# Whole-row loads and GpSimd-issued stores in place of paired-row loads and SP-issued stores, in a fused recurrent-unit and feed-forward kernel

## The chip, the cores and the metric

The kernel runs on one core of a Trainium2 chip. The metric is device time in microseconds (us), the median of several runs. The engines are named as in the profile: PE is TensorE, DVE is VectorE, ACT is ScalarE, POOL is GpSimd and SP is SyncE. A core moves data with 16 DMA engines; an engine's sequencer issues a transfer on its queue, and the transfer then runs beside the engines.

## The reference, cut to what matters

```
log_a = 8 * sigmoid(r_gate) * log(sigmoid(a_param))      # per channel
a     = exp(log_a)
g     = sqrt(max(1 - a*a, 1e-6)) * sigmoid(i_gate) * x
h[t]  = a[t] * h[t-1] + g[t]                             # over 5824 steps, 4 sequences
out   = (((h @ w1) * (h @ w2)) @ w3) @ w_out
```

The inputs x, r_gate and i_gate are float32 of 4 x 5824 x 256. The feed-forward weights are 256 x 1024 (w1, w2), 1024 x 1024 (w3) and 1024 x 256 (w_out). The output has 23,296 rows of 256 float32 numbers.

## The kernel before

**Chunks.** The 23,296 rows are worked through in 47 chunks: two of 256 rows, 44 of 512, and one of 256. The recurrence needs channels on partitions and time along the free dimension, while the inputs lie in memory with channels along a row. So each chunk is loaded by rows, the gate's tanh (`th_r`) and the gated input (`u_t`) are made in that layout as bf16, and both are turned. Chunks 0, 1, 2, 3, 4, 7 and 12 turn the gate on TensorE, and chunks 0 to 7 turn the input there (`turn_pe`, into PSUM tiles `ptr`); the others are turned by a DMA transpose that SP issues (`turn_dma`, L205, into `rt` and `ut`).

**Steps of a chunk.** In the order that data flows, with the letter that the kernel's order list uses:

- r, i, x (`load`, L142): three loads by SP, 512 KB each for a chunk of 512 rows.
- R, I (L150 and L160, ACT): tanh of both gates. p (L166, POOL): adds 1 to the input gate. t (L170, POOL, in two halves): multiplies it with x into `u_t`.
- V, U: the turns.
- d (`decay`, L209, ACT, once per 128 channels): `a_t` = exp of the turned gate. s (`square`, L220, POOL mostly): a times a into `nrm`. q (`root`, L230, ACT): the square root.
- g (`gated`, L235, DVE): `nrm` times the turned input. h (`scan`, L252, DVE, once per 128 channels): the recurrence, into `h_t`. y (`cast`, L267, POOL): `h_t` to bf16 `y_t`.
- a, b (L287 and L291, PE): the two up projections into PSUM. c (L302, ACT, some on DVE): a's result into `sa`. m (L308, DVE): the product with b's result, into `g_t`.
- D (`down`, L315, PE): the down projection, with w3 and w_out folded into one matrix at the start. e (`evac`, L327, ACT, some on DVE): the result from PSUM into `ot`, 256 rows at a time, in a ring of three tiles. o (`store`, L340): one transfer of 256 KB from `ot` to the output.

The last chunk has its own evacuation and store (`evac_last`, `store_last`, L331 and L336), in two transfers of 128 KB.

**Which rows lie where.** For chunks that both turns of which are on TensorE (`long_rows`: 0, 1, 2, 3, 4 and 7), a partition holds 4 (or 2) neighbouring rows, and decay and the gated product put time back in order with strided views. For all other chunks a partition holds pairs of neighbouring rows (`run(c)` is 2), that is, runs of 2 KB. After the turn the even and the odd rows then lie in separate blocks of 128 columns. `decay` reads these blocks densely and writes every second element of `a_t` (`paired`, `halves`). `gated` does the same in two instructions, one for each j, each of 128 x 512 elements for a chunk of 512 rows:

```
nc.sync.dma_start(
    out=t[:, :n, :].rearrange("p (h j) c -> p h j c", j=run(c)),
    in_=src[nm][starts[c]:starts[c] + sizes[c], :].rearrange("(h p j) c -> p h j c", p=P, j=run(c)))
...
a, pr = paired(a), halves(pr)
```

**Order of the work.** The kernel has its whole order written out by hand as a list of words (`ORDER`, L454). `o8.1` is the second store of chunk 8, `y11` the cast of chunk 11. Each word emits its instructions on its engine, and each engine and each queue works strictly in the order of the list. Waits between engines are made by semaphores, for data and for tiles of a ring that come free. So an instruction that waits holds up all that follow on its engine. Before the change, SP's queue carries everything that moves: loads, DMA transposes and stores.

Of the kernel before, what the change touches and what calls it, by code (L numbers as in the profile page):

```python
# [13 lines left out]
ALU = mybir.AluOpType  # L14
# [8 lines left out]
def kernel(  # L23
# [12 lines left out]
    nc = tc.nc  # L36
# [87 lines left out]
    def long_rows(c):  # L124
        return c in TURN_R and c in TURN_U

    def run(c):
        return sizes[c] // P if long_rows(c) else 2

    def paired(t):  # L130
        return t.rearrange("p (h q j) -> p h j q", q=P, j=2)

    def halves(t):
        return t.rearrange("p (h j q) -> p h j q", q=P, j=2)

# [6 lines left out]
    def load(c, nm):  # L142
        n = sizes[c] // P
        t = ring(loads, [P, 4, D], F32, name=nm + "_t", tag=nm)
        nc.sync.dma_start(
            out=t[:, :n, :].rearrange("p (h j) c -> p h j c", j=run(c)),
            in_=src[nm][starts[c]:starts[c] + sizes[c], :].rearrange("(h p j) c -> p h j c", p=P, j=run(c)))
        T[nm, c] = t
# [60 lines left out]
    def decay(c, cb):  # L209
# [4 lines left out]
        if long_rows(c):  # L214
            a, pr = in_time(a), turned(pr)
        else:
            a, pr = paired(a), halves(pr)
# [17 lines left out]
    def gated(c):  # L235
# [7 lines left out]
        for j in range(2):  # L243
            if w == CT:
                n = T["n", c].rearrange("p cb (x j) -> p j (cb x)", j=2)[:, j].rearrange("p (y q) -> p y q", q=P)
                pu = T["pu", c].rearrange("p cb (h j q) -> p j (cb h) q", q=P, j=2)[:, j]
            else:
                n = T["n", c][:, :, :w].rearrange("p cb (q j) -> p j cb q", j=2)[:, j]
                pu = T["pu", c][:, :, :w].rearrange("p cb (j q) -> p j cb q", q=P)[:, j]
            nc.vector.scalar_tensor_tensor(out=n, in0=n, scalar=1e-3, in1=pu, op0=ALU.max, op1=ALU.mult)  # L250
# [89 lines left out]
    def store(c, j2):  # L340
        t0 = starts[c] + 2 * j2 * P
        nc.sync.dma_start(out=out[t0:t0 + 2 * P, :].rearrange("(j p) c -> p j c", p=P),
                          in_=T["ot", c, j2])
# [89 lines left out]
    def last(c):  # L433
# [34 lines left out]
        b3.3 m3.2 m3.3 p5 a4.0.1 r9 a4.1.0 d5.0 d5.1 R8 d6.0 s6.0 s7.0 d6.1 p6 t5.0 p7 x6 x7 o0.0 a4.0.0 i10 V8 D2.0  # L468
        D2.1 c4.0.0 c4.1.0 b4.0 r10 o1.0 s5.0 s5.1 R9 s6.1 c4.0.1 s7.1 e2.0 m4.0 a4.2.0 a4.2.1 q7 V9 c4.2.0 a4.1.1
        c4.2.1 b4.1 t5.1 b4.2 c4.1.1 U5 a4.3.0 i8 o2.0 m4.1 D3.0 r11 t6.0 t6.1 U6 q5 q6 g5 h5.0 h5.1 c4.3.0 m4.2 i9 g6  # L470
        d8.0 a4.3.1 D3.1 D2.2 D2.3 b4.3 c4.3.1 d9.0 e3.0 y5 a5.1.0 t7.0 s8.0 b5.0 m4.3 e2.1 R10 d8.1 a5.0.0 a5.0.1
        h6.0 h6.1 a5.2.0 c5.1.0 D4.0 c5.0.0 c5.0.1 I8 m5.0 x8 a5.1.1 D4.1 c5.2.0 o3.0 I9 b5.1 a5.2.1 c5.1.1 b5.2 m5.1
        c5.2.1 R11 e4.0 p8 y6 m5.2 r12 I10 t7.1 a5.3.0 a6.0.0 U7 V10 c5.3.0 c6.0.0 d9.1 x10 r13 D3.2 g7 D3.3 e3.1
        a6.0.1 x9 t8.0 t8.1 a6.1.0 d10.0 d10.1 o2.1 V11 a6.1.1 a5.3.1 h7.0 h7.1 s9.0 c6.0.1 s9.1 c6.1.0 b6.0 R13 o4.0
        a6.2.1 a6.2.0 c5.3.1 c6.1.1 y7 m6.0 b5.3 s8.1 U8 D4.2 b6.1 a7.0.0 p9 p10 m5.3 t9.0 c6.2.0 b6.2 c6.2.1 R12 m6.1
        a6.3.0 q8 q9 D4.3 a6.3.1 c7.0.0 m6.2 c6.3.0 e4.1 t9.1 b6.3 c6.3.1 t10.0 t10.1 m6.3 V12 a7.0.1 g8 x11 h8.0 h8.1
        b7.0 a7.1.0 s10.0 d12.0 d12.1 c7.1.0 c7.0.1 D6.0 D6.1 m7.0 a7.2.0 D5.0 a7.1.1 D5.1 V13 d13.0 s13.0 i11 I11
        e6.0 o3.1 d11.0 y8 d11.1 e5.0 r15 c7.1.1 a7.2.1 b7.1 c7.2.0 c7.2.1 b7.2 U9 U10 i13 i12 r14 o4.1 x13 d13.1 o6.0
        a7.3.0 a7.3.1 a8.0.1 o5.0 m7.1 m7.2 R15 I13 a8.0.0 c8.0.0 b7.3 c8.0.1 c7.3.0 D6.2 c7.3.1 m7.3 p11 b8.1 s11.0
        D6.3 b8.0 a8.1.0 D5.2 D5.3 g9 h9.0 s10.1 s12.0 t11.0 i16 s11.1 R14 h9.1 e6.1 I12 c8.1.0 q10 p13 a8.1.1 c8.1.1  # L480
        m8.0 V15 q11 p12 y9 e5.1 m8.1 a8.3.0 D7.0 D7.1 V14 i15 o5.1 o6.1 r16 t13.0 t11.1 U11 r19 x12 a8.2.0 c8.2.0 g10
        h10.0 h10.1 c8.3.0 e7.0 y10 a8.2.1 d15.0 r17 b8.2 a8.3.1 b9.0 a9.0.0 c8.2.1 t13.1 m8.2 o7.0 x15 s15.0 a9.0.1
        D7.2 c8.3.1 c9.0.0 c9.0.1 I16 D7.3 m9.0 a9.1.0 d15.1 e7.1 b8.3 p16 a9.1.1 U13 m8.3 b9.1 a10.0.0 I15 a9.2.0
        c9.1.0 b9.2 c9.1.1 R16 a9.2.1 t12.0 p15 c10.0.0 d14.0 a9.3.0 a9.3.1 c9.2.0 s13.1 s14.0 d14.1 m9.1 D8.0 R17
        t12.1 c9.3.0 s12.1 c9.3.1 c9.2.1 V16 D8.1 D8.2 D8.3 a10.0.1 a10.2.0 m9.2 s15.1 e8.1 i14 r18 e8.0 c10.0.1 g11
        h11.0 h11.1 b10.0 a10.2.1 a10.1.0 y11 m10.0 b9.3 a10.1.1 b10.1 m9.3 c10.1.0 U12 x14 c10.2.0 d16.0 c10.1.1
        m10.1 d16.1 c10.2.1 a10.3.0 I14 a10.3.1 s16.0 b10.2 o8.1 s14.1 i19 c10.3.0 c10.3.1 R19 o7.1 a11.0.1 a11.0.0
        b10.3 t15.0 s16.1 a11.1.1 c11.0.0 c11.0.1 m10.2 m10.3 b11.0 x16 q12 m11.0 a11.1.0 c11.1.0 D10.0 a11.2.0 t15.1
# [136 lines left out]
```

## Time and profile before

| | |
|---|---|
| median of 3 runs | 521.21 us (520.61 to 521.88) |
| the profiled execution | 520.61 us, of which the profile's span is 518.8 us |
| granted TensorE clock | 1.0 |
| bytes moved by DMA | 123.82 MB, 239 GB/s in the mean |
| HBM read, written | 78.91 MB, 23.86 MB |
| median time to landing of a 512 KB load (r, i, x) | 5.4, 5.7, 5.4 us |
| median time to landing of a 256 KB store | 3.4 us |
| median time to landing of a DMA transpose | 4.4 us (rt), 4.3 us (ut) |

A row of the profile's groups reads: line, engine, operation, tile written and tiles read, shapes, count, then the busy time in us and the mean of one instruction in ns, then the idle time of the engine before these instructions and what ended it. A row of the waits reads: who waited for whom, us in total, times, and the longest. In the chain that ended last, the profile goes back from the last instruction to what released each one, and gives the share of the span by engine and line. A row of stretches reads: from and to, length, busy time and count of PE, weight loads, DVE, ACT and POOL, then the granted clock, the DMA engines' share and GB/s. Matmul ends are modelled, and matmuls overlap, so PE's busy time is not a measure of its peak.

The work of the start (loading weights and folding w3 with w_out) lasts until some 50 us; the first store is issued at 53.5 us and the last at 516.2 us.

### The profile page before, as it was taken

To read this page: it belongs to the slowest core of one execution; us is meant where nothing else is said; L and a number is where in the kernel's file an instruction comes from. 1 tells how busy PE (TensorE), PEld (TensorE's weight loads), DVE (VectorE), ACT (ScalarE), POOL (GpSimd) and SP (SyncE) were. 2 spreads that over 40 slices of the span, in tenths; PEclk is the share of its full clock that TensorE was granted. 3 is DMA by queue.
4 is the path that set the end of the run, shared out by engine and by line. 5 is a ranking of instruction groups with operands and counts; after the bars stand their busy time and mean duration, and the time that the engine had idled before them with its cause. 6 is when DMAs were issued, how large, how long until landed. Compare 5 with 4: busy or idle time off the path is not lost.

```text
span 518.8 us, 9105 instructions
## 1 busy us (share of the span) xinstructions
PE 501.7 (97%) x3267; PEld 313.9 (61%) x3321; DVE 443.1 (85%) x455; ACT 468.4 (90%) x720; POOL 310.2 (60%) x271
## 2 busy tenths in 40 slices
PE   7799999999999999999999999999999999999997
PEld 6658565566565566555656555565565655656566
DVE  4899999999999879989979699988989698859762
ACT  6999999999998999999999999998997969888553
POOL 1674858646637956866584993946645668480200
DMA  8996999999989998795998997989785896252112
GB/s 298 407 415 244 316 285 294 322 231 308 318 236 261 263 283 268 204 307 160 297 303 268 276 279 172 245 225 251 184 263 135 209 331 150 101 144 80 51 63 102
DMA packets 146178, 123.82 MB, mean 239 GB/s; under 512 B 86355, under 2 KB 110677, under 8 KB 146133
## 3 DMA queue, kind: packets, MB, share of 16 engines
q1 hardware_dynamic: 146128, 123.23, 82.6%
q8 instruction: 26, 0.43, 0.3%
q14 instruction: 20, 0.16, 0.1%
q10 hardware_dynamic: 4, 0.00, 0.0%
HBM read 78.91 MB, written 23.86 MB: 198 GB/s over the span
## 4 chain that ended last, share of the span: by engine, by line
PE 71%; ACT 10%; DVE 8%; DMA 5%; issue 4%; SPq 0%; ACTq 0%; DVEq 0%
PE po L323 24%; PE pb L284 23%; PE pa L284 22%; DMA wf<-in_moe_w_dram 4%; ACT sa L300 4%; DVE g_t L312 3%; DVE nrm L250 3%; ACT a_t L218 2%; DVE h_t L265 2%; PE pw L394 1%; DMA x_t<-in_x_dram 1%; ACT nrm L232 1%; ACT i_t L163 1%; ACT ot L300 1%; ACT th_r L156 1%
## 5 line engine op out<-in xcount | busy, mean ns | idle before, releaser
L312 DVE TENSOR_TENSOR g_t<-sa,pb 128x1024 bf16<-128x1024 bf16 (+1 forms) x188 | 218.5, 1179 | 53.5 <-PE pb L284 28.7
L284 PEld LDWEIGHTS <-w_sb 128*128 128x128 bf16 x1504 | 146.0, 98 | 152.1 <-issue 10.9
L300 ACT CAST sa<-pa 128x512 bf16<-128x512 f32 (+1 forms) x339 | 182.6, 589 | 30.3 <-PE pa L284 17.8
L284 PE MATMUL pa<-y_t,w_sb 128*128 128x512 bf16 (+1 forms) x721 | 185.9, 372 | 4.6 <-ACT sa L300 2.2
L284 PE MATMUL pb<-y_t,w_sb 128*128 128x512 bf16 (+1 forms) x729 | 182.7, 372 | 4.5 <-DVE g_t L312 2.6
L323 PE MATMUL po<-wp_sb,g_t 128*128 128x256 bf16 x1456 | 177.7, 273 | 0.6 <-ACT sa L300 0.3
L323 PEld LDWEIGHTS <-g_t 128*128 128x128 bf16 x1456 | 142.4, 98 | 40.6 <-issue 0.8
L274 POOL CAST y_t<-h_t 128x1024 bf16<-128x1024 f32 (+1 forms) x46 | 49.0, 1064 | 149.0 <-DVE h_t L265 116.0
L187 POOL TENSOR_TENSOR u_t<-i_t,x_t 128x512 bf16<-128x512 f32 (+1 forms) x89 | 121.7, 1384 | 6.9 <-DMA ut<-u_t 3.7
L265 DVE TENSOR_TENSOR_SCAN h_t<-a_t,h_t,nrm 128x512 f32<-128x512 f32 (+1 forms) x92 | 118.6, 1318 | 1.9
L228 POOL TENSOR_TENSOR nrm<-a_t 128x512 f32<-128x512 f32 (+1 forms) x74 | 81.0, 1113 | 13.2 <-ACT a_t L218 13.2
L250 DVE SCALAR_TENSOR_TENSOR nrm<-nrm,ut 128x512 f32<-128x512 f32 (+1 forms) x78 | 69.4, 931 | 5.6 <-ACT nrm L232 5.3
L218 ACT ACTIVATE a_t<-rt,la 128x512 f32<-128x512 bf16 (+1 forms) x80 | 67.8, 868 | 0.0
L168 POOL TENSOR_SCALAR i_t<-i_t 128x1024 f32<-128x1024 f32 (+1 forms) x45 | 51.1, 1138 | 17.9 <-ACT i_t L163 17.9
L300 ACT COPY ot<-po 128x512 f32<-128x512 f32 (+1 forms) x85 | 49.6, 591 | 11.0 <-PE po L323 10.8
L163 ACT ACTIVATE i_t<-i_t 128x1024 f32<-128x1024 f32 (+1 forms) x47 | 49.3, 1051 | 1.2 <-DMA i_t<-in_i_gate_dram 1.2
L232 ACT ACTIVATE nrm<-nrm 128x1024 f32<-128x1024 f32 (+1 forms) x47 | 48.3, 1040 | 0.2
L156 ACT ACTIVATE th_r<-r_t 128x1024 bf16<-128x1024 f32 (+1 forms) x40 | 42.6, 1066 | 0.0
L298 DVE CAST sa<-pa 128x512 bf16<-128x512 f32 (+1 forms) x37 | 21.8, 617 | 1.1 <-PE pa L284 0.9
L232 ACT ACT_TABLE_LOAD x17 | 21.8, 1283 | 0.3
L226 ACT ACTIVATE nrm<-a_t 128x512 f32<-128x512 f32 (+1 forms) x17 | 10.6, 647 | 0.1
L279 PE MATMUL warm<-ident 128*128 128x128 bf16 x128 | 10.3, 248 | 0.0
(57 smaller groups left out, 133.8 us busy)
## 6 DMA issues: line engine op xcount, KB each, us to landing
out_dram<-ot SPq DMA_DIRECT2D x90, 256.0 KB, 3.4
r_t<-in_r_gate_dram SPq DMA_DIRECT2D x44, 512.0 KB, 5.4
i_t<-in_i_gate_dram SPq DMA_DIRECT2D x44, 512.0 KB, 5.7
x_t<-in_x_dram SPq DMA_DIRECT2D x44, 512.0 KB, 5.4
wf<-in_moe_w_dram SPq DMA_DIRECT2D x12, 512.0 KB, 10.1
wf<-in_moe_w_out_dram SPq DMA_DIRECT2D x2, 512.0 KB, 10.4
r_t<-in_r_gate_dram SPq DMA_DIRECT2D x3, 256.0 KB, 3.0
i_t<-in_i_gate_dram SPq DMA_DIRECT2D x3, 256.0 KB, 4.8
```

The lines of the kernel that those rows point to most:

```text
L163: nc.scalar.activation(out=t[:, :n, :], in_=t[:, :n, :], func=AF.Tanh, scale=0.5)
L168: (nc.vector if c in DV_PLUS else nc.gpsimd).tensor_scalar(t, t, 1.0, 1.0, op0=ALU.add, op1=ALU.mult)
L187: (nc.vector if (c, half) in DV_HALF else nc.gpsimd).tensor_mul(out=u, in0=t, in1=xt)
L218: nc.scalar.activation(out=a, in_=pr, func=AF.Exp, scale=la4[:, cb:cb + 1], bias=la4[:, cb:cb + 1])
L228: (nc.vector if (c, cb) in DV_SQUARE else nc.gpsimd).tensor_mul(out=n, in0=a, in1=a)
L232: nc.scalar.activation(out=T["n", c][:, :, :w], in_=T["n", c][:, :, :w], func=AF.Sqrt, scale=-1.0, bias=1.0)
L250: nc.vector.scalar_tensor_tensor(out=n, in0=n, scalar=1e-3, in1=pu, op0=ALU.max, op1=ALU.mult)
L265: nc.vector.tensor_tensor_scan(h[:, cb, :], a[:, cb, :], n[:, cb, :], init, ALU.mult, ALU.add)
L284: nc.tensor.matmul(out=dst[:, :w], lhsT=w_sb[:, cb, m * P:(m + 1) * P], rhs=T["y", c][:, cb, :w], start=(cb == 0), stop=(cb == NCB - 1))
L300: nc.scalar.copy(out=dst, in_=src_ps)
L312: nc.vector.tensor_mul(out=T["g", c][:, 2 * mp:2 * mp + 2, :w], in0=T["sa", c, mp][:, :, :w], in1=T["pb", c, mp][:, :, :w])
L323: nc.tensor.matmul(out=po, lhsT=T["g", c][:, k, j * P:(j + 1) * P], rhs=wp_sb[:, k, :], start=(k == 0), stop=(k == KD - 1), skip_group_che ...
```

## The change

There are two edits.

First, chunks other than those of `long_rows` are loaded with whole rows spread over the partitions: row n x 128 + p goes to partition p. Each run in memory is one row, 1 KB, and after the turn time is in order. `decay` reads and writes densely; `gated` is one instruction for the whole chunk, 128 x 1024 for 512 rows. `long_rows` chunks are loaded as before.

Second, `store` is issued by POOL instead of SP. `store_last` stays on SP. In `ORDER` the words of the stores, and only these, are at other places: each stands ahead of a POOL word (p, t, s or y) that follows its evacuation, and the last six stand in the tail, where POOL has no other work.

```diff
-    def run(c):
-        return sizes[c] // P if long_rows(c) else 2
-
-    def paired(t):
-        return t.rearrange("p (h q j) -> p h j q", q=P, j=2)
-
-    def halves(t):
-        return t.rearrange("p (h j q) -> p h j q", q=P, j=2)
...
         nc.sync.dma_start(
-            out=t[:, :n, :].rearrange("p (h j) c -> p h j c", j=run(c)),
-            in_=src[nm][starts[c]:starts[c] + sizes[c], :].rearrange("(h p j) c -> p h j c", p=P, j=run(c)))
+            out=t[:, :n, :],
+            in_=src[nm][starts[c]:starts[c] + sizes[c], :].rearrange("(p n) c -> p n c" if long_rows(c) else "(n p) c -> p n c", p=P))
...
             a, pr = in_time(a), turned(pr)
-        else:
-            a, pr = paired(a), halves(pr)
...
-        for j in range(2):
-            if w == CT:
-                n = T["n", c].rearrange("p cb (x j) -> p j (cb x)", j=2)[:, j].rearrange("p (y q) -> p y q", q=P)
-                pu = T["pu", c].rearrange("p cb (h j q) -> p j (cb h) q", q=P, j=2)[:, j]
-            else:
-                n = T["n", c][:, :, :w].rearrange("p cb (q j) -> p j cb q", j=2)[:, j]
-                pu = T["pu", c][:, :, :w].rearrange("p cb (j q) -> p j cb q", q=P)[:, j]
-            nc.vector.scalar_tensor_tensor(out=n, in0=n, scalar=1e-3, in1=pu, op0=ALU.max, op1=ALU.mult)
+        nc.vector.scalar_tensor_tensor(
+            out=T["n", c][:, :, :w], in0=T["n", c][:, :, :w], scalar=1e-3,
+            in1=T["pu", c][:, :, :w], op0=ALU.max, op1=ALU.mult)
...
-        nc.sync.dma_start(out=out[t0:t0 + 2 * P, :].rearrange("(j p) c -> p j c", p=P),
+        nc.gpsimd.dma_start(out=out[t0:t0 + 2 * P, :].rearrange("(j p) c -> p j c", p=P),
                           in_=T["ot", c, j2])
...
-        c25.2.1 m25.0 m25.1 a25.3.0 a25.3.1 b25.2 o22.1 U28 b25.3 x32 R34 p30 a26.0.0 c25.3.0 V31 o23.0 h27.1 d29.1
-        t30.0 p29 t30.1 D24.0 D24.1 r37 o23.1 m25.2 r36 a26.0.1 c25.3.1 c26.0.0 R33 D24.2 p32 s32.1 c26.0.1 a26.1.0
...
-        c27.0.1 t32.0 a27.1.1 c27.1.0 o24.0 r40 i35 o24.1 c27.1.1 a27.3.1 q30 p31 p34 U29 h28.1 m27.0 i33 x34 b27.1
-        y28 a27.2.1 a27.3.0 D26.0 c27.2.1 c27.3.0 q29 b27.2 m27.1 m27.2 t32.1 o25.0 c27.3.1 U32 V33 q32 D26.1 b27.3
...
-        o44.1 o45.1 m46.2 m46.3 D46.0 D46.1 e46.0 e46.1 o46.0 o46.1
...
+        a25.1.0 d32.1 c25.0.1 c25.1.0 c25.1.1 o22.1 o23.0 y26 a25.2.1 d29.0 x31 h27.0 r33 i34 b25.0 b25.1 s30.0 s30.1
+        s32.0 a25.2.0 c25.2.0 c25.2.1 m25.0 m25.1 a25.3.0 a25.3.1 b25.2 U28 b25.3 x32 R34 o23.1 p30 a26.0.0 c25.3.0
...
+        a26.1.0 U30 s29.0 s29.1 y27 d31.0 D24.3 e24.0 b26.0 o24.0 t29.0 m25.3 e24.1 a26.2.0 a26.1.1 a26.2.1 I34
+        c26.1.0 b26.1 c26.2.0 V34 r35 c26.1.1 m26.0 g28 c26.2.1 I31 d31.1 b26.2 m26.1 m26.2 a26.3.1 a26.3.0 o24.1
...
+        t29.1 e25.0 c27.2.0 c27.0.1 t32.0 a27.1.1 c27.1.0 r40 i35 c27.1.1 a27.3.1 q30 p31 o25.0 p34 U29 h28.1 m27.0
...
+        e45.0 c46.3.0 c46.3.1 o44.0 e45.1 m46.2 m46.3 D46.0 D46.1 o44.1 e46.0 e46.1 o46.0 o46.1 o45.0 o45.1
```

## The prediction

> **What bounds the kernel now.** I read the page's busy times and its chain first, then the groups kept apart by shape, then the waits, and last GpSimd's timeline where it has least room.
>
> ```profile
> PE 501.7 (97%) x3267; PEld 313.9 (61%) x3321; DVE 443.1 (85%) x455; ACT 468.4 (90%) x720; POOL 310.2 (60%) x271
> ...
> PE 71%; ACT 10%; DVE 8%; DMA 5%; issue 4%; SPq 0%; ACTq 0%; DVEq 0%
> PE po L323 24%; PE pb L284 23%; PE pa L284 22%; DMA wf<-in_moe_w_dram 4%; ACT sa L300 4%; DVE g_t L312 3%; DVE nrm L250 3%; ACT a_t L218 2%; DVE h_t L265 2%; PE pw L394 1%; DMA x_t<-in_x_dram 1%; ACT nrm L232 1%; ACT i_t L163 1%; ACT ot L300 1%; ACT th_r L156 1%
> ```
>
> TensorE is the bound. Its records overlap, so I took starts instead: from one 128x512 matmul to the next 216 ns pass in the median, from one 128x256 to the next 109 ns. Between 40 and 500 us, what the starts lose against that pace is 17 us, and the quietest 20 us lose 0.43 already; above that floor stand 7.7 us in all. That **caps** what any help in the steady state can bring. DVE and ACT carry 18% of the chain. POOL and the store queue carry nothing: POOL costs something only if it makes TensorE wait for `y_t`.
>
> **Part 1, loads by whole rows.** Decay (L218) then writes densely, and the gated product (L250) is one 128x1024 instruction where two of 128x512 stood.
>
> ```profile
> L312 DVE TENSOR_TENSOR g_t<-sa,pb 128x1024 bf16<-128x1024 bf16 x176 | 210.4, 1213 | 46.7 <-PE pb L284 26.4 <-ACT sa L300 14.7 <-ACT a_t L218 1.9
> ...
> L250 DVE SCALAR_TENSOR_TENSOR nrm<-nrm,ut 128x512 f32<-128x512 f32 x76 | 68.7, 945 | 5.6 <-ACT nrm L232 5.3 <-DMA ut<-u_t 0.2
> L218 ACT ACTIVATE a_t<-rt,la 128x512 f32<-128x512 bf16 x78 | 66.6, 874 | 0.0
> ...
> L218 ACT ACTIVATE a_t<-ptr,la 128x512 f32<-128x512 bf16 x10 | 7.6, 790 | 0.1
> ```
>
> ```profile
> L250 DVE SCALAR_TENSOR_TENSOR nrm<-nrm,ut x78: 419/691/1760, 93.4 to 495.6; 128x512 f32<-128x512 f32 x76, 128x256 f32<-128x256 f32 x2
> ```
>
> The median L250 is 0.69 us, the mean 0.945: 23 of its 82 instructions take over 1 us, all while POOL works. Undisturbed, a pair costs 1.38 us and one 128x1024 about 1.21 (the L312 row), a saving of 0.17 of 1.89 us. If a long one is also held up only as often as a short one (23 of 82 by some 0.83 us, 0.23 on average), it costs 1.44 and saves 0.45. L250 holds 3.0% of the chain, 15.6 us, so the path gains 15.6 x 0.17/1.89 = 1.4 to 15.6 x 0.45/1.89 = 3.7 us. I take **-2.4**, nearer the middle, because POOL will be busier. For L218 the nearest rows are its PSUM form, 0.79 us, and no change, 0.874: 0 to 0.08 us off each. It holds 2% of the chain, 10 us, so 0 to 1 us; I take **-0.4**.
>
> [...]
>
> What part 1 costs is packets. By the trace's packet records a 2 KB packet takes 84 ns and a 1 KB packet 46 ns (medians). The loads of 40 chunks of 512 rows and one of 256 turn 31,104 packets of 2 KB into twice as many of 1 KB: 31,104 x 8 ns / 16 engines = 15.6 us more on each, 3% of the span.
>
> ```profile
> q1 hardware_dynamic: 146128, 123.23, 82.6%
> ```
>
> So 82.6% becomes about 86%, and a load lands some 0.5 us later than its 5.4. Loads land a median 10.6 us ahead of use, and four of the 111 that I could place within 0.3 us. I cost this at 0, hidden by that lead; without it, four loads of 0.5 us are +2.
>
> **Part 2, stores from POOL.** Ninety stores of 256 packets leave SP. They were its longest wait, and the loads and transposes behind them in SP's order go out sooner:
>
> ```profile
> SPq L342 <- ACT ot L300: 99.4, 32, 8.9
> ```
>
> Little compute waits for these: by the waits, ACT and DVE lose 5 us to DMA (2 of them at the end, to a store) and POOL 5.4, all but a few of these off the path. So 0 gained, 2 us at most; it pays for the later landings above. A store that left SP a mean 2.9 us after its evacuation now leaves POOL about 1 us after it, so the ring of three `ot` tiles comes free no later, while POOL keeps up.
>
> On POOL each store waits for its evacuation (ACT, some DVE) and behind it wait the jobs p, t, s and y. Of the 84 stores with a job behind them, 83 have their evacuation done before that job's recorded start; the wait itself costs nothing. The issue does. No POOL issue is in this trace; the nearest rows are SP's:
>
> ```profile
> L342 SPq DMA_DIRECT2D out_dram<-ot x90: 372/428/1274, 53.5 to 514.7; - x90
> ```
>
> ```profile
> L205 SPq DMA_TRANSPOSE rt<-th_r x40: 1189/1247/3352, 48.3 to 455.7; - x40
> ```
>
> A store takes SP 0.47 us (mean), a transpose with four times the packets 1.56. Call POOL's price g: 0.47 to 1.56; I take the middle, 1.0, as POOL's own rows are slower than other engines' for like work. Before 36 of the 84 following jobs POOL idles at least 1 us with the evacuation done (much of it waiting for the scan: 116 us), so there g is hidden; 40 jobs follow without idle time, and there it moves POOL back until its next pause. The tightest place:
>
> ```profile
> 260.00:300.00 40.00, 39.30 (x243) 24.02 (x246) 32.80 (x28) 38.60 (x61) 31.56 (x27) 1.00 1.01 281
> ```
>
> ```profile
> 283.59 1.04 POOL L274 CAST y_t<-h_t 128x1024 bf16<-128x1024 f32 x1 [4.84 <-DVE h_t L265]
> ...
> 302.78 1.04 POOL L228 TENSOR_TENSOR nrm<-a_t 128x512 f32<-128x512 f32 x1 [1.06 <-ACT a_t L218]
> ...
> 310.08 1.03 POOL L274 CAST y_t<-h_t 128x1024 bf16<-128x1024 f32 x1
> ```
>
> ```profile
> 313.34 1.03 PE L284 MATMUL pa<-y_t,w_sb 128*128 128x512 bf16 x4
> ```
>
> In the third row POOL is busy 31.56 of 40 us. From y26 (283.59) to y28's end (311.11) it pauses once, 1.06 us. Stores o22.1 and o23.0 now stand ahead of y26 from 281.95, and o23.1, o24.0, o24.1, o25.0 after it: y28 is late by (2g - 1.64) + 4g - 1.06 = 6g - 2.7 us, and TensorE asks for it 2.2 us after its recorded end. The loss is 6g - 4.9: nothing up to g = 0.82, **+1.1** at 1.0, 2.3 at 1.2. Walking all POOL jobs in the same way (start = recorded start, or the end of what is now ahead) finds no worse y up to 1.56, where backlog from before y26 adds and the loss is 6; lateness elsewhere (y20, y24) is no extra, since a TensorE already late by y28's amount finds its y there.
>
> **The end.** Last comes o46.1, still from SP: issued 516.24, landed 517.93. o45.1 is evacuated at 514.64; with g = 1.0 and the 1.7 us that SP's store took after its issue it lands at 517.3, hidden; at g = 1.56 it reaches 517.9. Cost 0.
>
> **Sum:** -2.4 - 0.4 + 1.1 = -1.7 us. The profiled execution took 520.61 (span 518.8 and 1.8 around it), 0.6 below the median; I apply the change to the median: **519.5 us**.
>
> **Rivals.** *The gains and the POOL delay cancel* (g about 1.2 to 1.35, +2.3 to 3.2 against -2.8, or part 1 at its low end): 520.2 to 522.2. For it: both terms are small and uncertain. *POOL becomes the bound, slower than before:* price g per store, decisive from g of about 1.4, where the walk's 4.1 passes the gain of 2.8 by over 0.2%. At 1.56, 521.2 - 2.8 + 6 = 524.5. At 2.0 POOL has 310 + 180 = 490 busy us, its pauses no longer catch up, and the walk leaves y43 18 us late: 536. For it: eight stores share 8.4 idle us at 260 to 300. Against it: the whole span has 208 idle us for 90 stores, 2.3 each. [...] *The DMA engines fall behind:* they stand at 1.00 and above of their time between 60 and 140 us; the 3% of extra packets is then 2 to 4 us by 180 us, and if leads there (2 us for several r and i loads) do not absorb it, 522.5 to 525. Against it: SP is freed of 110 us of waits. *Part 1 does not do what it says* (L250 collides as before): that is the low end above, 520.5 at g = 1.0.
>
> **How the numbers follow.** About 0.2% (1.04 us) is what a measurement of this kernel tells from no change. Forecast 0.42 (faster, below 520.17); cancelled, with part 1's failure, 0.22 (same); POOL bound 0.22 and DMA behind 0.14 (slower, 0.36). Low end: -3.7 - 1.0 and no POOL loss give 516.5, and I go to 515.5, the rest of the 7.7 cap being unlikely. High end: 6 at g = 1.56 with the DMA's 2 and only the smaller gain is 528, and so is g = 1.8 by the walk (10 us); half of the way from there to the 536 of g = 2.0 is 532. Less than 2 in 10 lie outside. Forecast alone: 515.5 to 520.2.
>
> **What would show it.** POOL's `out_dram` group gives g. L250 should count 41 instructions near 1.2 to 1.45 us, L218 fall below 0.86, q1's 2 KB packets vanish. A wait of `pa` L284 for `y_t` L274 near 310 us beyond 2 us, POOL busy above 85%, or long waits of ACT or POOL for loads would make the forecast wrong.

## The result, and the profile after

The changed kernel takes **548.98 us** (median of 4 runs, 548.18 to 552.63) beside 521.12 us for the kernel before in the same comparison: a ratio of 1.0547, with a 95% interval of 1.0498 to 1.0596. The forecast was 519.5 us, with a range up to 532. The change costs 28 us where I expected a gain of 2. Times below are medians of all runs; the ratios leave out one slow run each of `e2_pool_only` and `e8_act_queue`.

Line numbers shift with the edit: the scan is now L249 (before L265), the gated product L232 (L250), decay L207 (L218), the product into `g_t` L296 (L312), the cast L258 (L274), the up projections L268 (L284), the store L326 (L342). From the page of the changed kernel, span 547.3 us: the busy times, the two large DMA queues, the chain by engine.

```profile
PE 507.5 (93%) x3267; PEld 315.3 (58%) x3321; DVE 467.2 (85%) x414; ACT 467.2 (85%) x720; POOL 372.6 (68%) x361
...
q1 hardware_dynamic: 152752, 99.63, 66.6%
q0 software_dynamic: 7200, 23.60, 12.0%
...
PE 49%; ACT 16%; DVE 16%; issue 11%; DMA 5%; POOL 2%; SPq 0%; DVEq 0%; ACTq 0%
```

TensorE's share of the chain falls from 71% to 49%; what takes its place is ACT, DVE and "issue". POOL still has only 2%. DVE does 41 instructions fewer than before and is busy 24 us longer. The groups kept apart by shape say where:

```profile
L249 DVE TENSOR_TENSOR_SCAN h_t<-a_t,h_t,nrm 128x512 f32<-128x512 f32 x88 | 141.2, 1634 | 1.9
...
L232 DVE SCALAR_TENSOR_TENSOR nrm<-nrm,ut 128x1024 f32<-128x1024 f32 x38 | 68.6, 1806 | 5.4 <-ACT nrm L221 5.4
L326 POOL DMA_DIRECT2D out_dram<-ot x90 | 67.3, 748 | 59.4 <-ACT ot L284 54.9 <-ACT sa L284 3.8 <-issue 0.4
L207 ACT ACTIVATE a_t<-rt,la 128x512 f32<-128x512 bf16 x78 | 62.9, 823 | 2.3 <-DMA rt<-th_r 2.3
```

A store costs POOL 0.748 us, less than the 1.0 that I took. Decay fell to 0.823 us as hoped. But the scan, which the change does not touch, went from a mean of 1.345 to 1.634 us, and the long gated product takes 1.8 and not 1.44. The scan before:

```profile
L265 DVE TENSOR_TENSOR_SCAN h_t<-a_t,h_t,nrm 128x512 f32<-128x512 f32 x88 | 115.7, 1345 | 1.9
```

Shortest, median and longest, from the views of the source lines: the scan before, the scan after, and the gated product after:

```profile
L265 DVE TENSOR_TENSOR_SCAN h_t<-a_t,h_t,nrm x92: 726/1276/2117, 14.2 to 497.7; 128x512 f32<-128x512 f32 x88, 128x256 f32<-128x256 f32 x4
```

```profile
L249 DVE TENSOR_TENSOR_SCAN h_t<-a_t,h_t,nrm x92: 725/1277/9492, 13.9 to 525.0; 128x512 f32<-128x512 f32 x88, 128x256 f32<-128x256 f32 x4
```

```profile
L232 DVE SCALAR_TENSOR_TENSOR nrm<-nrm,ut x39: 684/1225/5869, 95.6 to 522.6; 128x1024 f32<-128x1024 f32 x38, 128x512 f32<-128x512 f32 x1
```

The medians (1.277 and 1.225 us) are those of undisturbed instructions. A few took up to 9.5 us. Not every DVE instruction is held up: of the 188 products into `g_t`, one input of which lies in PSUM, the longest took 1.222 us, 1.223 before. The longest scan, first what POOL did around it, then DVE (start, duration, engine and line):

```profile
443.32 1.47 POOL L326 DMA_DIRECT2D out_dram<-ot  x2
444.83 1.06 POOL L159 TENSOR_SCALAR i_t<-i_t 128x1024 f32<-128x1024 f32 x1
445.85 2.03 POOL L217 TENSOR_TENSOR nrm<-a_t 128x512 f32<-128x512 f32 x2
447.85 2.05 POOL L159 TENSOR_SCALAR i_t<-i_t 128x1024 f32<-128x1024 f32 x2
...
452.09 1.03 POOL L217 TENSOR_TENSOR nrm<-a_t 128x512 f32<-128x512 f32 x1
453.09 3.39 POOL L178 TENSOR_TENSOR u_t<-i_t,x_t 128x512 bf16<-128x512 f32 x2
```

```profile
445.93 9.49 DVE L249 TENSOR_TENSOR_SCAN h_t<-a_t,h_t,nrm 128x512 f32<-128x512 f32 x1
```

The scan starts behind two stores and ends at 455.42, after POOL has gone through eight jobs. The `g_t` product behind it on DVE starts only then, and TensorE waits 6.4 us for it, until 456.6.

To put a size on this I compared every scan and gated product with its undisturbed duration (1.26 us for a scan of 512, 1.22 and 0.69 for a gated product of 1024 and 512) and added up what lay over 0.15 us. TensorE's stalls by starts are the time by which matmuls start later than 216 or 109 ns (for 512 or 256 columns) after the one before:

| kernel | held up, us in all | up to 1.15 us | over 1.15 us | longest | TensorE's stalls by starts, us |
|---|---|---|---|---|---|
| before | 26.0 | 38 | 0 | 1.07 | 28.0 |
| after | 54.8 | 31 | 11 (35.3 us) | 8.23 | 55.5 |

Before, a scan or gated product is held up by one POOL job at most (1.07 us). After, eleven are held up for longer, and each of the eleven has a store of POOL zero to three jobs earlier in the same unbroken run of jobs. In seven of them DVE gets in as the run of jobs ends or comes to its last job; in the other four (at 210.7, 278.4, 301.6 and 366.2 us) it gets in where POOL comes to a further store. By the releases, the stalls of `pb` for `g_t` alone grow from 5.3 to 22.4 us; the stalls in all grow by 27.5, as does the time (27.9). Some 4 us of this are not waits but a slower pace: around the end of TensorE's two longest stalls (at 171.0 and 456.6 us) its granted clock is 0.5 for a while (3.4 and 6.8 us), and 18 of the 128x512 matmuls there start 427 ns apart and not 216. The stretch of the second, before and after (the clock is the third number from the end):

```profile
420.00:460.00 40.00, 38.80 (x236) 23.46 (x240) 32.88 (x30) 34.95 (x57) 28.34 (x24) 1.00 0.63 186
420.00:460.00 40.00, 32.45 (x183) 18.33 (x184) 35.80 (x23) 27.69 (x45) 31.06 (x28) 0.94 0.65 197
```

The waits show TensorE's side before, and POOL's and TensorE's after (total, times, longest):

```profile
PE pb L284 <- DVE g_t L312: 2.6, 5, 0.9
```

```profile
POOL out_dram L326 <- ACT ot L284: 54.9, 24, 4.3
...
PE pb L268 <- DVE g_t L296: 19.3, 9, 6.3
```

### The profile page after: what moved, and what is told of

The parts are those of the page before. It is cut to its first block, busy times and chain, and to the rows that moved or that the text cites. A ratio compares the mean times of both kernels' runs of the same rounds, so it can differ in the third digit from the quotient of the medians.

```text
span 547.3 us, 9073 instructions
## 1 busy us (share of the span) xinstructions
PE 507.5 (93%) x3267; PEld 315.3 (58%) x3321; DVE 467.2 (85%) x414; ACT 467.2 (85%) x720; POOL 372.6 (68%) x361
## 4 chain that ended last, share of the span: by engine, by line
PE 49%; ACT 16%; DVE 16%; issue 11%; DMA 5%; POOL 2%; SPq 0%; DVEq 0%; ACTq 0%
PE po L307 16%; PE pb L268 16%; PE pa L268 15%; DVE g_t L296 7%; ACT sa L284 5%; DVE nrm L232 4%; DVE h_t L249 4%; DMA rt<-th_r 3%; ACT a_t L207 2%; DMA r_t<-in_r_gate_dram 2%; ACT i_t L154 2%; ACT ot L284 2%; ACT nrm L221 2%; ACT L221 1%; PE pw L378 1%
## 5 line engine op out<-in xcount | busy, mean ns | idle before, releaser
L296 DVE TENSOR_TENSOR g_t<-sa,pb 128x1024 bf16<-128x1024 bf16 (+1 forms) x188 | 218.2, 1178 | 56.8 <-PE pb L268 26.5
L268 PEld LDWEIGHTS <-w_sb 128*128 128x128 bf16 x1504 | 147.4, 99 | 177.7 <-issue 38.7
L284 ACT CAST sa<-pa 128x512 bf16<-128x512 f32 (+1 forms) x339 | 182.3, 586 | 50.8 <-DVE g_t L296 25.6
L268 PE MATMUL pb<-y_t,w_sb 128*128 128x512 bf16 (+1 forms) x729 | 185.1, 376 | 21.1 <-DVE g_t L296 19.3
L268 PE MATMUL pa<-y_t,w_sb 128*128 128x512 bf16 (+1 forms) x721 | 189.5, 377 | 9.4 <-ACT sa L284 5.0
L249 DVE TENSOR_TENSOR_SCAN h_t<-a_t,h_t,nrm 128x512 f32<-128x512 f32 (+1 forms) x92 | 144.1, 1595 | 1.9
L178 POOL TENSOR_TENSOR u_t<-i_t,x_t 128x512 bf16<-128x512 f32 (+1 forms) x89 | 119.2, 1351 | 0.8
L258 POOL CAST y_t<-h_t 128x1024 bf16<-128x1024 f32 (+1 forms) x46 | 50.7, 1102 | 90.3 <-DVE h_t L249 76.3
L326 POOL DMA_DIRECT2D out_dram<-ot x90 | 67.3, 748 | 59.4 <-ACT ot L284 54.9
L217 POOL TENSOR_TENSOR nrm<-a_t 128x512 f32<-128x512 f32 (+1 forms) x74 | 77.4, 1063 | 11.2 <-ACT a_t L207 10.8
L232 DVE SCALAR_TENSOR_TENSOR nrm<-nrm,ut 128x1024 f32<-128x1024 f32 (+1 forms) x39 | 69.3, 1777 | 5.4 <-ACT nrm L221 5.4
L207 ACT ACTIVATE a_t<-rt,la 128x512 f32<-128x512 bf16 (+1 forms) x80 | 64.0, 817 | 2.3 <-DMA rt<-th_r 2.3
L284 ACT COPY ot<-po 128x512 f32<-128x512 f32 (+1 forms) x85 | 49.5, 589 | 12.7 <-PE po L307 12.5
L159 POOL TENSOR_SCALAR i_t<-i_t 128x1024 f32<-128x1024 f32 (+1 forms) x45 | 52.3, 1163 | 5.9 <-ACT i_t L154 5.4
```

Of the source, the lines that this page charges most:

```text
L178: (nc.vector if (c, half) in DV_HALF else nc.gpsimd).tensor_mul(out=u, in0=t, in1=xt)
L207: nc.scalar.activation(out=a, in_=pr, func=AF.Exp, scale=la4[:, cb:cb + 1], bias=la4[:, cb:cb + 1])
L217: (nc.vector if (c, cb) in DV_SQUARE else nc.gpsimd).tensor_mul(out=n, in0=a, in1=a)
L232: nc.vector.scalar_tensor_tensor(out=T["n", c][:, :, :w], in0=T["n", c][:, :, :w], scalar=1e-3, in1=T["pu", c][:, :, :w], op0=ALU.max, op1 ...
L249: nc.vector.tensor_tensor_scan(h[:, cb, :], a[:, cb, :], n[:, cb, :], init, ALU.mult, ALU.add)
L268: nc.tensor.matmul(out=dst[:, :w], lhsT=w_sb[:, cb, m * P:(m + 1) * P], rhs=T["y", c][:, cb, :w], start=(cb == 0), stop=(cb == NCB - 1))
```

## The experiments

Theory A, formed on these traces: behind a DMA that POOL issues, POOL's jobs no longer let DVE in between, so DVE's instructions on SBUF wait for POOL's run of ready jobs to end. Rivals: the stores' new places in the order; POOL's time and its waits; the output ring. "Before" beside each run is the kernel before, run in the same comparison.

### Each part alone

`e1_rows_only` keeps the new loads and puts the stores back, on SP and at their old places in `ORDER`:

```
-        nc.gpsimd.dma_start(out=out[t0:t0 + 2 * P, :].rearrange("(j p) c -> p j c", p=P),
+        nc.sync.dma_start(out=out[t0:t0 + 2 * P, :].rearrange("(j p) c -> p j c", p=P),
```

> Part 1 alone: whole-row loads, stores by SP at their old places. Theory A (a DMA issued by POOL makes POOL keep DVE out over several jobs): no scan longer than about 2.2 us, L250's successor at 1.2 to 2.1 us, 518 to 521 us. Rival C (the 128x1024 gated product or the doubled packets lose the time): about 545 us, with scans and gated products of 3 us and more. Rival D (places of the stores): 518 to 521 us, as A.

Measured: **516.97 us** (516.0 to 518.1) beside 519.79: ratio 0.9941 [0.992, 0.9962]. This version beats both kernels, and none of the later ones does better. Its groups and queue:

```profile
L207 ACT ACTIVATE a_t<-rt,la 128x512 f32<-128x512 bf16 x78 | 63.2, 829 | 0.0
L232 DVE SCALAR_TENSOR_TENSOR nrm<-nrm,ut 128x1024 f32<-128x1024 f32 x38 | 54.2, 1426 | 6.7 <-ACT nrm L221 5.2 <-DMA ut<-u_t 1.4
```

```profile
q1 hardware_dynamic: 177232, 123.23, 85.5%
```

The gated product at 1.43 us, decay at 0.83, the DMA engines at 85.5%: part 1 did what was predicted.

`e2_pool_only` does the reverse: the paired loads of the kernel before, the changed `store` and `ORDER`.

> Part 2 alone: paired-row loads as before, stores by POOL at their new places. Theory A: several scans or gated products of 3 to 9 us, each in a run of POOL jobs that has a POOL DMA shortly before; 540 to 555 us. Rival C: about 521 us, none of them over 2.2 us. Rival D: 540 to 550 us, as A.

Measured: 557.14 us, ratio 1.0688 [1.0625, 1.0751]. Fifteen DVE instructions are held up over 1.15 us (44.8 us), and 69.0 us are held up in all. The loss is part 2's. It is larger than the changed kernel's, and so are the hold-ups; what adds to them, with two gated products per chunk instead of one, was not taken apart.

### Places, POOL's time, and the DMA itself

`e3_sp_new_places` is the changed kernel with its stores issued by SP, at the new places (the edit of `e1_rows_only`, with the new `ORDER`).

> The changed kernel with its stores issued by SP at the new places in the order. Theory A: no scan over 2.2 us; 518 to 524 us. Rival B (POOL's backlog): as A, since POOL issues nothing here. Rival D (the new places hold SP up, or rings come free late): 535 us or more.

`e4_copy_for_dma` adds to that a POOL job at each store's place, which waits for the same evacuation and takes about as long (0.871 us in the mean and 0.612 in the median, against 0.748):

```
+        junk = ring(ffn, [P, 2, D], BF16, name="junk", tag="junk")
+        nc.gpsimd.tensor_copy(out=junk, in_=T["ot", c, j2])
         nc.sync.dma_start(...)
```

> The changed kernel, but where POOL issued a store it now copies the ot tile to a scratch tile of bf16 (128x512, an ordinary job of about 0.65 us with the same wait for the evacuation), and SP issues the store after it. The copy is extra work that the result does not need. Theory A: POOL is as late as with the DMAs, but DVE's two-input instructions wait for one POOL job at most: scans up to about 2.2 us, 519 to 526 us. Rival B (a POOL with a backlog of ready jobs keeps DVE out, whatever made the backlog): scans of 4 to 9 us, 540 to 555 us.

Measured: `e3_sp_new_places` 527.55 us, 1.0128 [1.0088, 1.0168]; `e4_copy_for_dma` 531.76 us, 1.0235 [1.0184, 1.0286]. Both lie between the ranges that I had given for theory A and for its rival. The steps from `e1_rows_only` are: places 10.6 us, a POOL job of about the store's length with its waits (46.4 us of them for evacuations, 54.9 in the changed kernel) 4.2, and POOL's DMA in place of that job and of SP's DMA 17.2. Held up, in the measure of the table above, are 13.6, 13.9 and 25.9 us in the three, none over 1.15, against 54.8 in the changed kernel. With the copies DVE is held up more often than in the changed kernel, 57 times against 42, but by one job each time.

The cost of the places was new to me. With them, `pa` stalls 5.5 us for the evacuation into `ot`, ACT waits 4.0 us for a store to free an `ot` tile, and the span ends 4.6 us after the last matmul instead of 3.1. SP's own waits for evacuations grow too:

```profile
SPq L326 <- ACT ot L284: 93.3, 31, 9.9
...
SPq L326 <- ACT ot L284: 129.8, 45, 7.0
```

The first row is of `e1_rows_only`, the second of `e3_sp_new_places`. All this is on SP; how much of it the changed kernel pays on POOL's queue, these two runs can't say.

`e10_fourth_tile` asks whether the output ring is to blame: the changed kernel with `"ot": 4` in place of `"ot": 3`.

> The changed kernel with a fourth output tile and nothing else; the stores stand where the change put them. It parts the two edits of the run with the stores ahead of the y casts. Theory A (the stores stand ahead of unpaused runs of GpSimd jobs, and behind them VectorE is kept out): the runs are the same, so it stays at 540 to 549 us, with VectorE's long instructions still held up over several jobs. Rival D (the late release of the three output tiles is the cause, and the fourth tile was what helped there): 526 to 532.

Measured: 547.58 us, 1.0532 [1.0467, 1.0596], twelve long hold-ups (36.8 us). The ring of three tiles is not the cause.

`e7_before_y` has the fourth tile too, and moves 82 of the stores directly ahead of a `y` word, where POOL mostly pauses for the scan (76.3 us in all in the changed kernel):

```
-        ... b3.3 m3.2 m3.3 o0.0 p5 a4.0.1 r9 a4.1.0 ...
-        ... s7.0 d6.1 p6 t5.0 o1.0 p7 x6 x7 a4.0.0 ...
+        ... b4.3 c4.3.1 d9.0 e3.0 o0.0 o1.0 o2.0 y5 a5.1.0 ...
```

> The changed kernel with a fourth ot tile and 82 of the stores directly ahead of a y cast, where POOL mostly pauses for the scan. Theory A: after such a store POOL pauses, so few runs of products follow a DMA; blocked time of scans and gated products falls from 56 to under 30 us, 520 to 532 us. If a pause sets nothing right: as the changed kernel, 545 to 555 us.

Measured: 528.36 us, 1.0158 [1.0129, 1.0187], with two long hold-ups (5.9 us). All 90 stores are still POOL's; only their places, and so what stands behind them, differ from `e10_fourth_tile`, and 19 us come back.

`e8_act_queue` tries the third queue: `e1_rows_only` with `nc.scalar.dma_start` in `store`.

> Whole-row loads with the stores of 256 KB issued by ACT on its own queue at the places of the kernel before. Theory A: DVE as free as with SP's stores (no scan over 2.2 us). ACT is busy 90% of the span, and each issue takes some of its time (about as SP's 0.4 us, 36 us for 90): 518 to 530 us. If ACT's issue costs nothing and SP's waits mattered, below 516 us.

Measured: 541.24 us, 1.0385 [1.0342, 1.0428], slower than I expected. DVE is held up no more than in `e1_rows_only` (13.0 us), and an issue takes ACT's sequencer 0.38 us. But an ACT store leaves only when ACT has come to its word: the trace has ACT idle 19.6 us for stores to free their `ot` tiles (eight times, up to 4.5 us), which `e1_rows_only` has not among its waits.

`e5_drain` was to break the run by a drain: `nc.gpsimd.drain()` behind each store of the changed kernel.

> The changed kernel with a drain of POOL behind every store that POOL issues. Theory A1 (after a DMA parts of POOL run ahead of others, so that at the end of a job not all of it lets go; a drain brings them together): no scan over 2.4 us, and the time of the copy in place of the DMA, 527 to 534 us. Rival A2 (the descriptor writing or the transfer itself shuts DVE out): scans of 3 to 9 us stay, 545 to 560 us.

Measured: 741.8 us, 1.4254 [1.4208, 1.4301], far off. No hold-up is over 1.08 us, as theory A wants, but POOL stands still for at least 1.88 us behind every store (307.6 us in all between a store and the next job, against 73.1 in the changed kernel), and `pa` on TensorE waits 133 us for `y_t`. A drain is no cure, and the run says nothing of the size of the effect.

### The effect by itself

`e6_alone` is a program of its own, as are three further ones below, each read from one execution. POOL issues a store, or something else, then works through seven multiplications of 128x512 without a pause, and DVE is given one scan of 128x512 early in that run.

```
        if kind in ("dma", "drain", "pause"):
            nc.gpsimd.dma_start(out=rows, in_=src)
...
        for k in range(JOBS):
            pj = sb.tile([P, 512], F32, name=f"job_{kind}", tag=f"job_{kind}_{k}")
            nc.gpsimd.tensor_mul(out=pj, in0=first, in1=vb)
...
        nc.vector.tensor_tensor_scan(h, later, vb, 0.0, ALU.mult, ALU.add)
```

> The collision by itself; nothing of the reference is computed, and the output is only partly written. 72 cases of seven ready POOL products (128x512) with one DVE scan of two SBUF inputs that starts 0.6, 1.7 or 2.7 us after the run of products is let go. Ahead of the products POOL has nothing (scan_none), a copy (scan_copy), a DMA of 256 KB (scan_dma), that DMA and a drain of POOL (scan_drain), or that DMA and then a pause of 2 us or more (scan_pause); or SP issues the DMA (scan_spdma). Theory A (POOL's DMA makes the jobs behind it keep DVE out until POOL pauses): scan_dma reaches 5 to 9 us, scan_none, scan_copy and scan_spdma stay at 2.4 us or less, and so does scan_pause. If the drain sets POOL right, scan_drain also stays at 2.4. Rival B (any run of ready jobs does it): scan_none and scan_copy are as long as scan_dma.

Its groups by shape (mean in ns, 12 cases each):

```profile
L98 DVE TENSOR_TENSOR_SCAN scan_dma<-later,vb 128x512 f32<-128x512 f32 x12 | 110.4, 9201 | 126.2 <-ACT later L96 126.2
...
L98 DVE TENSOR_TENSOR_SCAN scan_none<-later,vb 128x512 f32<-128x512 f32 x12 | 21.7, 1808 | 114.2 <-ACT later L96 114.2
L98 DVE TENSOR_TENSOR_SCAN scan_pause<-later,vb 128x512 f32<-128x512 f32 x12 | 21.5, 1789 | 179.9 <-ACT later L96 179.9
```

Behind a POOL store the scan takes 9.2 us; without a store, 1.8; with the same store issued by SP, 1.8; with a POOL copy instead, 1.5; with POOL's store and then a pause, 1.8; with POOL's store and then a drain, 1.2. The jobs of POOL are the other side of it: 1259 ns in the mean behind the store, where they never give way, and 1393 without it.

`e9_what_it_takes` varies the number of jobs, the size of the store, the kind of POOL job and the DVE instruction.

> A program of its own, which computes nothing of the reference: 80 small cases in a row. In each, GpSimd issues a store of 256 KB (in `small` 32 KB, in `onefree` none) and then works through 4, 7 or 12 jobs of 128x512 without a pause; VectorE is given one instruction of 128x512 about 0.6 or 1.7 us after the jobs began. Theory A (behind a store of its own, GpSimd keeps out a VectorE instruction with two SBUF inputs until its run of ready jobs ends): the scan ends with the run, so it lasts a mean of about 6 us with four jobs, 9 to 10 with seven, 14 to 16 with twelve; the size of the store is no matter (`small` 9 to 10); a plain product with two SBUF inputs (`mul`) waits as the scan does, 8 to 9.5; an instruction with one input (`one`) does not wait and equals `onefree`, below 0.8. Jobs with one input (`plusone`) were among those passed in the changed kernel, so 9 to 10 there too. Rival B (the wait is tied to the transfer, its descriptors or its landing some 4 us later): seven and twelve jobs give the same, at most 6, and `small` is short. Rival C (GpSimd keeps everything of VectorE out): `one` waits like the scan.

```profile
L93 DVE TENSOR_TENSOR_SCAN dve_twelve<-later,vb 128x512 f32<-128x512 f32 x10 | 158.0, 15800 | 31.5 <-ACT later L86 31.5
...
L93 DVE TENSOR_TENSOR_SCAN dve_seven<-later,vb 128x512 f32<-128x512 f32 x10 | 89.0, 8900 | 22.5 <-ACT later L86 22.5
L89 DVE TENSOR_SCALAR dve_one<-later 128x512 f32<-128x512 f32 x10 | 89.0, 8900 | 31.9 <-ACT later L86 31.9
...
L93 DVE TENSOR_TENSOR_SCAN dve_plusone<-later,vb 128x512 f32<-128x512 f32 x10 | 14.2, 1417 | 31.5 <-ACT later L86 31.5
```

The DVE instructions came a little earlier than planned, most of them from 0.5 us before the first job's start to 0.6 us after it. The hold-up grows with the run: 6.1 us in the mean with four jobs (not shown), 8.9 with seven, 15.8 with twelve. So nothing that the transfer does ends it; the end of the jobs does. A store of 32 KB does the same as one of 256 KB (8.7). Two of my expectations fell. The DVE instruction with one SBUF input (`dve_one`, float32) waits just as long, against 1.3 us without a store. That is the sign I had given for rival C; against it stand the products into `g_t` in the kernel, which have an input in PSUM and were not held up, also where two of them ran beside and right behind two stores (2.48 us for both, from 443.53). And POOL jobs of one input, in the form tried here (1.54 us each), let the scan in after 1.4. In the changed kernel the jobs of L159, also of one input but some 1.03 us for twice the elements, are among those that passed. What tells these two forms apart stays open. Three of the 60 cases with a store and two-input jobs were short. One of them (1.23 us) says nothing, as its scan began 0.2 us ahead of the store; the other two (1.22 and 0.69) escaped though POOL had no pause, so the effect is not certain each time.

`e11_how_long_a_pause` lets the first job wait for ScalarE, later and later.

> A program of its own, which computes nothing of the reference: 84 small cases. In each, GpSimd issues a store of 256 KB and then works through seven jobs of 128x512, and VectorE is given a scan of 128x512 about 1.7 us after the first job became ready. In `p0` the jobs wait for nothing; in `p1` to `p6` the first of them waits for ScalarE, which is done from about 0.3 us before the end of GpSimd's store instruction to about 1.4 us after it. Theory A, that it takes an unpaused run behind the store: `p0` and `p1`, without a pause, hold the scan to the end of the seven jobs (mean 8 us or more), and from some pause of a few tenths of a us on the scan takes below 2.5 us, as in the earlier case with a pause of 2 us. If only the transfer's own progress counts (rival B, some 4 us to landing), all pauses shorter than that hold the scan as `p0` does. If the mere wait on a semaphore breaks the run, `p1` is already below 2.5.

By POOL's records, `p0` to `p3` had no pause (0.02 us between store and job in the median) and the scan took 9.2, 8.7, 7.9 and 7.8 us in the mean; `p4` had 0.15 us, `p5` 0.57 and `p6` 1.23, and the scan took 2.75, 2.14 and 2.14. Case by case it parts cleanly: in all 46 with 0.02 us the scan was held up (8.4 to 9.5 us), in all 36 with 0.11 us or more it was let in (1.3 to 2.2), and of two at 0.08 and 0.10 us one went each way. A semaphore that is already there breaks nothing; some 0.11 us of pause does.

`e12_what_cuts_it` puts a small POOL instruction between the store and the seven jobs.

> A program of its own, which computes nothing of the reference: 84 small cases, each a store of 256 KB by GpSimd, then a small instruction of GpSimd that differs from case to case, then seven jobs of 128x512 without a pause, and a scan of 128x512 on VectorE about 1 to 2 us after the first job began. `bare` has no small instruction, `set` a memset of 128x1, `sets` three of them, `wideset` a memset of 128x512, `tiny` and `tinies` one and three copies of 128x1, `plus` a one-input addition of 128x128. Theory A (any run without a pause holds the scan, however it begins): all of them hold it to the end of the seventh job, a mean of 6 to 8.5 us. Rival E (the state behind a store ends when GpSimd executes a cheap instruction, or one that reads little): those cases fall to the 2 us that the scan took behind a pause.

```profile
L99 DVE TENSOR_TENSOR_SCAN scan_set<-later,vb 128x512 f32<-128x512 f32 x12 | 98.3, 8193 | 45.6 <-ACT later L97 45.6
L99 DVE TENSOR_TENSOR_SCAN scan_bare<-later,vb 128x512 f32<-128x512 f32 x12 | 96.8, 8070 | 51.3 <-ACT later L97 51.3
...
L99 DVE TENSOR_TENSOR_SCAN scan_sets<-later,vb 128x512 f32<-128x512 f32 x12 | 14.7, 1225 | 140.2 <-ACT later L97 140.2
```

One memset of 128x1 changes nothing, nor does a wide memset, a copy of 128x1 or an addition (8.2 to 8.7 us). Three memsets of 128x1 free the scan wholly: 1.23 us in all twelve cases; three copies of 128x1 do nearly (1.48). It is not the delay: the addition and the wide memset put the jobs off by longer (0.5 us against 0.4), and no pause among the three is over 0.06 us. Theory A as I had put it, any run without a pause, is too strong: why a few tiny instructions in a row free the scan is not shown here.

### The cut, in the kernel

`e13_three_memsets` puts that behind each store of the changed kernel, `e14_memsets_before_y` behind each store of `e7_before_y`:

```
         nc.gpsimd.dma_start(out=out[t0:t0 + 2 * P, :].rearrange("(j p) c -> p j c", p=P),
                           in_=T["ot", c, j2])
+        for _ in range(3):
+            nc.gpsimd.memset(dot, 0.0)
```

> The changed kernel with three memsets of 128x1 on GpSimd behind each of its 90 stores, and nothing else. The memsets cost GpSimd some 0.4 us each time, 35 us in all, and its stores still wait for the evacuations. Theory A (VectorE's being kept out makes up most of the loss): no long VectorE instruction is held up over more than one job, the product that waits for it costs TensorE a few us instead of 22, and the time falls to 528 to 536 us, near the kernel with a copy in place of each store. Rival F (the loss lies in GpSimd's time, in the waits behind the stores or in the queue): more work on GpSimd makes it 549 or more.

> The kernel with four output tiles and each store directly ahead of a y cast, with the three memsets behind each store. There only two VectorE instructions were still held up over more than one job, 5.9 us in all. Theory A: 524 to 530 us, the memsets giving back what is left of that and costing y casts up to 0.4 us each; below 517 it would beat the kernel with the loads alone, which I don't expect. Rival F: 530 to 540.

Measured: `e13_three_memsets` 540.48 us (538.82 to 541.91), 1.038 [1.0338, 1.0422]. With POOL busy 46 us longer the kernel is 8.5 us faster than the changed one. The eleven long hold-ups are gone (none over 1.07 us, 31.4 in all), and `pb`'s stalls for `g_t` fall from 22.4 to 6.0 us. That is theory A in the kernel itself. The time stays above my 528 to 536, and below the 549 of rival F; its page shows what the memsets cost:

```profile
PE 505.1 (94%) x3267; PEld 314.9 (59%) x3321; DVE 444.4 (83%) x414; ACT 467.8 (87%) x720; POOL 418.6 (78%) x631
```

DVE gets 23 us back; POOL is busy 46 us longer, 28.5 in memsets and nearly all the rest in jobs that take longer again (`u_t` 1.49 us in the mean, against 1.37 in the changed kernel and 1.42 in `e1_rows_only`). POOL has 14% of the chain, where it had 2%. `e14_memsets_before_y` shows a price without the gain: 546.42 us, 1.0496 [1.0468, 1.0524], above both ranges that I had given and 18 us slower than `e7_before_y`, which had only 5.9 us of long hold-ups to give back. The waits of `pa` for `y_t` there rise from 3.8 to 13.3 us. So POOL's time, rival F, counts too where a `y` stands right behind; what makes up the rest of the 18 us I did not take apart.

## Why the prediction was wrong, step by step

**The bound and the cap hold.** TensorE was the bound, and `e1_rows_only`, the part of the change that helps, gained 0.6%, 3.1 us of the capped 7.7.

**Part 1 was right, in sign and size.** Predicted -2.4 - 0.4 = -2.8 us; measured -0.59% of 519.79, -3.1 us, with an interval of -4.2 to -2.0. The long gated product was put between 1.72 and 1.44 us (savings of 0.17 and 0.45 on the pair's 1.89) and took 1.426; decay between 0.79 and 0.874, and took 0.829. By the prediction's own shares of the chain these two are worth -3.8 and -0.5 us, a little beyond the interval, so that -2.8 came so near is in part luck: the value in the middle was taken because POOL would be busier, which it is not in `e1_rows_only`. The DMA engines were put at 86% and stood at 85.5%; loads landed 0.1 to 0.3 us later where I allowed 0.5, and it cost nothing that shows. Of the two cases that the prediction weighed for the long product, the mean of 1.426 speaks for the better one, a long one held up only about as often as a short one (put at 1.44).

**POOL's price per store was mis-sized, to the safe side.** g is 0.748 us (0.725 to 0.904), not 1.0. By the prediction's own 6g - 4.9 the loss at y28 is then nothing, and the trace agrees as far as it can: TensorE's stalls for `y_t` are 1.4 us in all by the releases (1.2 before), and near y28 `pa` waits 1.8 us at most, put down to ACT. With the right g my sum would have been 518.4 us, further off than with the wrong one. (In the sum at g = 1.56, 521.2 - 2.8 + 6 makes 524.4 and not 524.5, which changes nothing.) The rival with POOL as the bound, which needed a g of about 1.4 or more, did not come: no issue took over 0.904 us beside a DVE that was busy 85% of the time. DVE is the one that is held up, by 8.23 us at the longest.

**The step that failed** is the sentence "POOL costs something only if it makes TensorE wait for `y_t`", and with it "the wait itself costs nothing. The issue does." I priced a store as time on its own engine. Its main price was on another: behind it, DVE instructions that work in SBUF alone wait for POOL's run of ready jobs (eleven of them for over 1.15 us, 35.3 us together). The trace of before showed the mild form of this, DVE held up by one POOL job, 26.0 us in all and never over 1.07 us, and I used it for the gated product; I took its size to be the same after the change. It is 54.8, and TensorE gets it through `g_t`, for which `pb` stalls 22.4 us, 5.3 before. The wait itself came out otherwise too: POOL waits 54.9 us for evacuations in 24 waits, where I had 83 of 84 stores find theirs done. That this is the smaller part the copies show, which wait 46.4 us and cost 4.2.

The size: 17.2 us by `e4_copy_for_dma` against the changed kernel, a step that also moves the stores from SP's queue to POOL's; and 8.5 by `e13_three_memsets`, net of what 46 us of POOL time cost there. The changed order made it worse than it had to be: more than half of the stores stood ahead of a p, t or s job, and many had others right behind, the arrangement that gives long unbroken runs. `e7_before_y` shows that with the stores elsewhere most of it goes.

**The second step that failed** is "the ring of three `ot` tiles comes free no later, while POOL keeps up". SP's stores at the new places cost 10.6 us against the old ones, with stalls for evacuations and `ot` tiles. In the changed kernel itself the ring is worth little (the fourth tile: 1.4 us, within the intervals), so how much of the 10.6 is paid there, and how much on SP's queue alone, remains open.

**SP's freedom** was put at 0 to 2 us gained, "it pays for the later landings". Loads landed later than in `e1_rows_only` all the same, 6.0 to 6.2 us after issue against 5.5 to 5.8, and nothing shows a gain. **The end** was put at 0: from the last matmul to the span's end there are 4.2 us, 3.1 before, so some 1.1 us of loss.

**What I had named as signs of being wrong** did not appear: POOL is busy 68%, not 85, and `pa` waits for `y_t` once, for 1.3 us. Here is the stretch that I had found tightest, whose row was shown for before:

```profile
260.00:300.00 40.00, 37.46 (x241) 23.63 (x243) 37.26 (x27) 37.34 (x59) 30.68 (x29) 1.00 0.93 253
```

The fifth of the busy times, POOL's, is no higher than before (30.68 after 31.56). The third is the one that I was not watching: DVE's, 37.26 after 32.80, with one instruction fewer.

**What is shown and what is argued.** Shown: the hold-up, what it takes (a DMA issued by POOL, then two-input jobs without a pause), that in the programs of its own it ends with the run, that a pause of 0.11 us or more or three tiny instructions undo it, and that undoing it in the kernel brings time back. Not shown: the mechanism, why the one-input jobs of `e9_what_it_takes` let DVE in, and why the granted clock falls around the longest stalls. Before, one POOL job at most held a scan or gated product up (1.07 us); the 9.49 us scan behind two stores sat through eight. What POOL's issue changes, so that DVE does not get in at the end of a job, is not measured, and no run here looks inside POOL. The picture that the expectation of `e5_drain` gives for theory A1 was a guess of mine: that a drain, a pause or three tiny instructions free DVE would fit it, but does not show it, and it doesn't explain the one-input jobs.

## What to carry to other kernels

Before a DMA is moved to POOL's queue, look at what POOL does right behind it and what DVE does at that time: with jobs ready behind the store, DVE's work in SBUF can wait for all of them (15.8 us in the mean for a scan behind a store and twelve jobs, `e9_what_it_takes`), and neither POOL's busy time nor any wait on POOL shows it (in the changed kernel POOL was busy 68% and had 2% of the chain). Look at the longest duration of a group and not at its median (9.49 us and 1.277 for the scan); here the time for which DVE was held up counted as DVE's busy time. If POOL must issue, place the store where POOL pauses afterwards (528.36 us in `e7_before_y`); here SP was the better queue even with 93 us of its own waits for evacuations (516.97 us in `e1_rows_only`).

## What the runs showed of the hardware

- Behind a DMA issued by POOL, a DVE instruction of 128x512 in SBUF took 8.1 to 15.8 us in the mean beside seven to twelve jobs, and 1.3 to 2.1 us where the store was SP's, absent, or followed by a pause of some 0.5 us or more; with stores of 32 and 256 KB it took 8.7 and 8.9 us (`e6_alone`, `e9_what_it_takes`, `e11_how_long_a_pause`, `e12_what_cuts_it`). In the changed kernel the products into `g_t`, with one input in PSUM, were not held up (1.222 us at most).
- A float32 DVE instruction with a single SBUF input was held up as long as one with two (8.9 us, 1.3 without a store; `e9_what_it_takes`).
- A pause of 0.11 us or more between the store and the jobs, or three memsets of 128x1 (0.43 us), freed DVE (in all of 36 and 12 cases); one memset (0.1 us) or one of 128x512 did not (8.2 and 8.6 us; `e11_how_long_a_pause`, `e12_what_cuts_it`).
- POOL's issue of a 256 KB store took 0.748 us in the changed kernel, against 0.43 for SP's before (medians); it went out as packets of 4 KB, and landed after 4.4 us, against 3.4 for SP's.
- A drain on POOL behind a store stopped it for at least 1.88 us in the kernel (`e5_drain`).
- In the changed kernel, around the end of stalls of TensorE of 4.7 and 6.4 us its granted clock was 0.5 for 3.4 and 6.8 us, and 128x512 matmuls started 427 ns apart and not 216.
